# A one-core attention, expert and gated MLP kernel: exponential table and row sums of the first tiles, and the order of two accumulations

## The chip, the core and the metric

The kernel runs on one core of a Trainium2 chip. The metric is the device time of one execution in microseconds; the figure for a kernel is the median of its runs. The profile shows one such execution, instruction by instruction, on the five engines: TensorE (PE in the rows; its weight loads are PEld), VectorE (DVE), ScalarE (ACT), GpSimd (POOL) and SyncE (SP), which issues the DMAs.

## What is computed

Three stages follow each other, all in float32, on 2304 tokens of width 512 (18 tiles of 128 tokens):

```
attention, in chunks of 64 tokens, 8 heads of width 64:
    scores = q @ k.T / 8;  scores -= max(scores);  attn = exp(scores)
    attn /= sum(attn) + 1e-9;  x = attn @ v
experts, 4 of them, width 1024, p = probs normalised per token:
    out += p[:, e] * (relu(x @ w1[e]) @ w2[e])
gated MLP, width 1536:
    xn = x / sqrt(mean(x * x) + 1e-6) * rms_g
    out = (silu(xn @ w_gate) * (xn @ w_val)) @ w_out
```

## The kernel before

The 18 token tiles are worked in three sets of six. Within a set, two blocks of three tiles (384 tokens) are the columns of the first products. Every float32 matrix is split into a high and a low float32r part, and a product is the sum of three matmuls: high by high, high by low, low by high (PASSES). In the code and in the rows, hh and hl are the two parts of the hidden activations, w the two parts of a weight tile, x those of the input.

**First products.** All but the very first use a scheme with seven products per pair of chunks in place of eight (hidden, from line 738): a_ps, b_ps, d_ps and c_ps are the PSUM banks of its partial results, VectorE adds them up (line 198, a helper), ScalarE applies Relu and writes hh (line 796), VectorE writes hl (line 799). In the gated MLP VectorE multiplies by the silu (line 830), ScalarE writes hh (line 833), and hl comes from GpSimd, or, for the last chunk of the first block, from VectorE (line 197, a helper). That last chunk is the bank d_ps, the last product to end. The first set's first pair of chunks is done plainly instead (plain, bank c_ps).

**Second products.** After every two pairs of chunks (fps, k = 0 and 1, each with two chunks j) outer runs over the six token tiles t. For each tile it takes one PSUM bank, o, and adds up 12 matmuls of 128x512 (line 856): six for the pair k = 0, then six for k = 1. Then flush moves the bank out: VectorE scales it and adds it into acc (line 1049; 1047 the first time) in the expert stage, or adds it into out in the gated MLP. I call one run of outer a pass. There are 33, of 72 matmuls each: 8 for each set in the expert stage (24), 3 for each set in the gated MLP (9). They are numbered from 0.

**Lead-in.** Before the first pass the six attention tiles of the first set are computed one by one (attention_unit with first_softmax), between the plain products of the first two pairs of chunks. For a tile TensorE makes the scores (sc), VectorE takes row maxima (line 616) and the negative bias nb (line 620), ScalarE makes the exponentials, four for each half (line 625, accum_out gives the row sums as well), VectorE turns the sums into reciprocals (lines 631 and 632), GpSimd multiplies (at, line 635), TensorE transposes (trA, line 521), ScalarE copies (aT, line 526), TensorE multiplies with v (pv, line 544), and ScalarE and VectorE write the parts of x (lines 560, 197 and 571). In the same stretch ScalarE and GpSimd split the first weights, which arrive as r from in_w (ScalarE's casts are lines 315 and 356, GpSimd's subtractions line 197). TensorE fills some idle time with transposes into a bank called scratch (line 959).

**What sets the order.** The program is recorded in one go, engine by engine, in the order in which the Python code issues it; each engine then works through its own list in order. In the lead-in Chains.race decides that order: each generator says before a step which engine it needs and for how many microseconds (the dictionary in yield) and which of its own earlier steps it follows (the number), and the step that could begin first is issued first. So an estimate changed in first_softmax moves other instructions as well. Later, work.tick lets background chains (weight preparation, attention of the next sets) issue steps between the products, by a running clock. PSUM banks are handed out in the order in which they came free (Banks).

Of the kernel before, what the change touches and what calls it, by code (L numbers as in the profile page):

```python
# [8 lines left out]
F32 = mybir.dt.float32  # L9
# [3 lines left out]
AF = mybir.ActivationFunctionType  # L13
ALU = mybir.AluOpType
AX = mybir.AxisListType
# [3 lines left out]
P = 128  # L19
CH = 64  # L20

PASSES = ((0, 0), (0, 1), (1, 0))
# [128 lines left out]
def fused_kernel(ctx, tc, qkv, probs, w12, wglu, gvec, out):  # L151
# [4 lines left out]
    nc = tc.nc  # L156
# [455 lines left out]
    def first_softmax(sc, ex, att):  # L612

        mx, nb, rs = (sm.tile([P, 2, HP], F32, tag=f"f{n}", name=n) for n in ("mx", "nb", "rs"))
        for h2 in range(2):
            nc.vector.tensor_reduce(
                mx[:, h2, :].unsqueeze(2), sc[h2][:, :HP * CH].rearrange("p (g n) -> p g n", n=CH), axis=AX.X, op=ALU.max
            )
            yield {"DVE": 0.45 if h2 == 0 else 0.2}, 1
        nc.vector.tensor_scalar(nb, mx, -SCALE, None, op0=ALU.mult)  # L620
        for h2 in range(2):
            yield {"ACT": 0.9}, 1
            for g in range(HP):
                cols = slice(g * CH, (g + 1) * CH)
                nc.scalar.activation(  # L625
                    ex[h2][:, cols], sc[h2][:, cols], AF.Exp, scale=SCALE, bias=nb[:, h2, g:g + 1],
                    accum_out=rs[:, h2, g:g + 1],
                )
            banks.put(sc[h2])
        yield {"DVE": 0.5}, 1  # L630
        nc.vector.tensor_scalar_add(rs, rs, 1e-9)
        nc.vector.reciprocal(rs, rs)
        for h2, e in enumerate(ex):
            yield {"POOL": 0.65}, 1
            nc.gpsimd.tensor_tensor(
                att.rearrange("p (hp r n) -> p hp r n", hp=HP, r=2)[:, :, h2, :],
                e[:, :HP * CH].rearrange("p (g n) -> p g n", n=CH),
                rs[:, h2, :].unsqueeze(2).to_broadcast([P, HP, CH]),
                op=ALU.mult,
            )  # L640
            tp.put(e)
# [78 lines left out]
    def bank(name):  # L720
        if not banks.free():
            work.force(None, banks.free)
        return banks.get(name)
# [122 lines left out]
    def outer(fps, w2, flush, aside):  # L846

        catch_up()
        for t in range(TPS):
            b, r = divmod(t, TPB)  # L850
            ps = bank(f"o_{t}")
            last = (len(fps) - 1, 1, len(PASSES) - 1)
            for k, fp in enumerate(fps):
                for j in range(2):
                    for m, (hx, wi) in enumerate(PASSES):
                        nc.tensor.matmul(  # L856
                            ps, hs[fp, b, j][hx][:, r * P:(r + 1) * P], w2[2 * k + j][:, wi],
                            start=((k, j, m) == (0, 0, 0)), stop=((k, j, m) == last),
                        )
                if k == len(fps) - 1:  # L860
                    flush(t, ps)
                    banks.put(ps)
                work.tick(6 * 0.227)
                aside(t * UF + k)
        for fp in fps:
            for b in range(2):
                for j in range(2):
                    hi, lo = hs.pop((fp, b, j))
                    hh.put(hi)
                    hl.put(lo)  # L870
        w2p.put(*w2)
# [53 lines left out]
    with tc.manual_schedule():  # L925
        units = [[i, i + 1] for i in range(0, NTILE, 2)]
        own = lambda s: units[s * TPS // 2:(s + 1) * TPS // 2]
        make_identity(nc, ident)
        fetching = work.add(fetch())
        lead = [[i] for i in range(TPS)]  # L930
        tiles = [attention_tiles(u) for u in lead]
# [201 lines left out]
```

## Time and profile before

| | |
|---|---|
| median of 3 runs | 1246.94 us (1246.8 to 1248.53) |
| the profiled execution's own time | 1249.17 us |
| its span, first to last instruction | 1247.4 us |
| mean granted TensorE clock | 0.997 of full speed |
| PE busy, DVE busy, POOL busy, ACT busy | 1223.3, 783.0, 537.4, 449.0 us |

In timeline rows the first number is the start in microseconds from the beginning of the span, the second how long the group of instructions took, then engine, line, operation, what is written and read, shape, and how many instructions the row merges; in square brackets stands how long the engine had been idle and what ended that. A matmul's own duration is longer than the distance to the next one, since matmuls are pipelined; starts tell the pace.

### The profile page before, as it was taken

How to read it: one execution, taken by the hardware profiler on the slowest of the kernel's cores; microseconds unless marked ns; L12 is line 12 of the kernel's file. 1: busy time of each engine (PE TensorE's matmuls, PEld its weight loads, DVE VectorE, ACT ScalarE, POOL GpSimd, SP SyncE). 2: the span in 40 equal slices, each digit the busy share in tenths (PEclk: the TensorE clock that was granted, in tenths of full speed). 3: DMA queues.
4: the chain of work that ended last, by engine and by line, in shares of the span. 5: the costliest groups of instructions: out<-in, count | busy, mean ns of one | idle time of the engine just before them, and what ended most of it. 6: DMA issues, size and time to landing. Idle time of an engine off the chain costs nothing.

```text
span 1247.4 us, 20675 instructions
## 1 busy us (share of the span) xinstructions
PE 1223.3 (98%) x7253; PEld 1107.0 (89%) x7253; DVE 783.0 (63%) x1388; ACT 449.0 (36%) x1109; POOL 537.4 (43%) x575
## 2 busy tenths in 40 slices
PE   7999999999999999999999999999999999999998
PEld 6888899989997987889999999998998998998997
DVE  3765444456776787677677766786766634763644
ACT  7454333334243233333244224333435341332211
POOL 3696666654463563526355445354313101130100
PEclk9999999999999999999999999999999999999999
DMA  8377455554577697755667677657956935855843
GB/s 293 106 255 284 173 194 186 187 202 157 191 253 250 235 326 262 243 169 207 224 235 269 201 243 252 201 164 259 311 194 233 304 112 197 285 189 186 302 131 124
DMA packets 140215, 274.05 MB, mean 220 GB/s; under 512 B 16208, under 2 KB 16208, under 8 KB 140112
## 3 DMA queue, kind: packets, MB, share of 16 engines
q1 hardware_dynamic: 140112, 272.73, 64.0%
q8 instruction: 58, 0.95, 0.3%
q14 instruction: 45, 0.37, 0.1%
HBM read 210.28 MB, written 62.39 MB: 219 GB/s over the span
## 4 chain that ended last, share of the span: by engine, by line
PE 77%; DVE 8%; POOL 5%; issue 4%; ACT 3%; DMA 2%; SPq 0%; POOLq 0%; DVEq 0%
PE o L856 36%; PE d_ps L706 11%; PE a_ps L706 11%; PE c_ps L706 11%; PE b_ps L706 6%; POOL w L197 3%; DMA w1m<-w 2%; DVE silu L830 2%; POOL tw L197 1%; DVE c_ps L198 1%; PE pv L544 1%; DVE u L198 1%; ACT e L625 1%; PE xT L911 1%; PE sc L497 1%
## 5 line engine op out<-in xcount | busy, mean ns | idle before, releaser
L856 PE MATMUL o<-w,hh 128*128 128x512 f32 x1584 | 492.8, 392 | 5.3 <-ACT hh L796 3.5
L856 PEld LDWEIGHTS o<-w,hh 128*128 128x128 f32 x1584 | 295.7, 188 | 69.4 <-ACT hh L796 5.2
L856 PE MATMUL o<-w,hl 128*128 128x512 f32 x792 | 311.5, 393 | 2.2 <-DVE hl L799 1.2
L197 POOL TENSOR_TENSOR w<-r,w 128x512 fp32r<-128x512 f32 (+1 forms) x146 | 163.4, 1127 | 135.5 <-ACT w L356 76.7
L706 PE MATMUL c_ps<-x,w 128*128 128x384 f32 x1080 | 216.2, 336 | 0.3 <-ACT e L625 0.3
L706 PE MATMUL d_ps<-x,w 128*128 128x384 f32 x984 | 198.6, 336 | 2.4 <-DVE c_ps L198 2.2
L706 PE MATMUL a_ps<-x,w 128*128 128x384 f32 x984 | 198.6, 336 | 0.9 <-ACT p L759 0.9
L706 PEld LDWEIGHTS c_ps<-x,w 128*128 128x128 f32 x1080 | 188.8, 188 | 0.8 <-ACT e L625 0.5
L856 PEld LDWEIGHTS o<-w,hl 128*128 128x128 f32 x792 | 148.9, 188 | 39.2 <-DVE hl L197 4.7
L1049 DVE SCALAR_TENSOR_TENSOR acc<-o,pr,acc 128x512 f32<-128x512 f32 x126 | 94.3, 749 | 135.0 <-PE o L856 134.7
L197 POOL TENSOR_TENSOR hl<-silu,hh 128x384 fp32r<-128x384 f32 x54 | 54.4, 1030 | 288.4 <-ACT hh L833 288.3
L706 PEld LDWEIGHTS a_ps<-x,w 128*128 128x128 f32 x984 | 173.4, 188 | 3.9 <-ACT p L759 1.2
L706 PEld LDWEIGHTS d_ps<-x,w 128*128 128x128 f32 x984 | 172.1, 188 | 4.4 <-DVE c_ps L198 4.3
L198 POOL TENSOR_TENSOR w<-w,sc 128x512 f32<-128x512 f32 x36 | 47.1, 1309 | 163.0 <-DVE sc L415 139.8
L197 POOL TENSOR_TENSOR w<-tw,w 128x256 fp32r<-128x256 f32 x112 | 87.2, 787 | 39.9 <-ACT w L231 34.2
L198 DVE TENSOR_TENSOR u<-b_ps,p 128x384 f32<-128x384 f32 x82 | 45.5, 554 | 88.2 <-PE b_ps L706 46.4
L706 PE MATMUL b_ps<-x,w 128*128 128x384 f32 x492 | 99.0, 335 | 0.0
L759 ACT COPY p<-a_ps 128x384 f32<-128x384 f32 x82 | 39.5, 482 | 162.4 <-PE a_ps L706 162.3
L796 ACT ACTIVATE hh<-c_ps 128x384 fp32r<-128x384 f32 x100 | 49.1, 494 | 131.9 <-DVE c_ps L198 130.3
L198 DVE TENSOR_TENSOR u<-c_ps,u 128x384 f32<-128x384 f32 x82 | 45.6, 556 | 74.1 <-PE c_ps L706 73.5
L231 ACT CAST w<-tw 128x256 fp32r<-128x256 f32 x112 | 42.6, 406 | 136.0 <-POOL tw L197 91.4
L706 PEld LDWEIGHTS b_ps<-x,w 128*128 128x128 f32 x492 | 86.4, 188 | 0.1
(109 smaller groups left out, 1346.5 us busy)
## 6 DMA issues: line engine op xcount, KB each, us to landing
w<-wgv SPq DMA_DIRECT2D x252, 256.0 KB, 3.9
w<-w1m SPq DMA_DIRECT2D x224, 256.0 KB, 5.2
r<-in_w SPq DMA_DIRECT2D x128, 256.0 KB, 4.8
w1m<-w SPq DMA_DIRECT2D x112, 256.0 KB, 2.5
wgv<-w SPq DMA_DIRECT2D x84, 256.0 KB, 4.7
raw<-in_wglu SPq DMA_DIRECT2D x36, 512.0 KB, 3.8
w<-wou SPq DMA_DIRECT2D x36, 512.0 KB, 7.4
wou<-q SPq DMA_DIRECT2D x24, 256.0 KB, 4.4
```

The lines of the kernel that those rows point to most:

```text
L197: sub = lambda eng, o, a, b: eng.tensor_tensor(o, a, b, op=ALU.subtract)
L198: add = lambda eng, o, a, b: eng.tensor_tensor(o, a, b, op=ALU.add)
L231: nc.scalar.copy(halves(out[n])[:, 0], at[part_of[n]])
L497: nc.tensor.matmul(sc[h2][c * CH:(c + 1) * CH, n:n + CH], q, k, start=True, stop=True)
L544: nc.tensor.matmul(ps[n][lo:lo + CH, o:o + CH], vt[a][lo:lo + CH, hp, ch, :], aT[a][lo:lo + CH, q:q + CH], start=True, stop=True,)
L625: nc.scalar.activation(ex[h2][:, cols], sc[h2][:, cols], AF.Exp, scale=SCALE, bias=nb[:, h2, g:g + 1], accum_out=rs[:, h2, g:g + 1],)
L706: nc.tensor.matmul(ps[:, :NB], wv[:, wi, k, :], xs[n][:, xi, k, :], start=(first and k == 0 and m == 0), stop=(last and k == KH - 1 and m ...
L759: nc.scalar.copy(p1, v(a))
L796: nc.scalar.activation(hi, src, AF.Relu)
L830: nc.vector.tensor_tensor(v, ps[:, :NB], v, op=ALU.mult)
L856: nc.tensor.matmul(ps, hs[fp, b, j][hx][:, r * P:(r + 1) * P], w2[2 * k + j][:, wi], start=((k, j, m) == (0, 0, 0)), stop=((k, j, m) == last),
L1049: nc.vector.scalar_tensor_tensor(out=acc[i], in0=ps, scalar=pr[:, i, e:e + 1], in1=acc[i], op0=ALU.mult, op1=ALU.add,)
```

## The change

Three things are edited. In first_softmax the exponentials no longer give row sums; instead VectorE adds up each half of a tile (a new TENSOR_REDUCE for each half, 12 in all), with estimates of their own for the race. Ahead of everything, a value of one element per partition is set to zero by VectorE and passed through Exp on ScalarE. In outer, the first two token tiles take turns: tile 0 with the pair k = 0, tile 1 with k = 0, tile 0 with k = 1, tile 1 with k = 1, with two banks open; the other four tiles stand as before.

```diff
             for g in range(HP):
                 cols = slice(g * CH, (g + 1) * CH)
                 nc.scalar.activation(
-                    ex[h2][:, cols], sc[h2][:, cols], AF.Exp, scale=SCALE, bias=nb[:, h2, g:g + 1],
-                    accum_out=rs[:, h2, g:g + 1],
+                    ex[h2][:, cols], sc[h2][:, cols], AF.Exp, scale=SCALE, bias=nb[:, h2, g:g + 1]
                 )
             banks.put(sc[h2])
-        yield {"DVE": 0.5}, 1
+        for h2 in range(2):
+            yield {"DVE": 0.4 if h2 == 0 else 0.8}, 2 - h2
+            nc.vector.tensor_reduce(
+                rs[:, h2, :].unsqueeze(2), ex[h2][:, :HP * CH].rearrange("p (g n) -> p g n", n=CH), axis=AX.X, op=ALU.add
+            )
         nc.vector.tensor_scalar_add(rs, rs, 1e-9)
...
     def outer(fps, w2, flush, aside):

         catch_up()
-        for t in range(TPS):
+        last = (len(fps) - 1, 1, len(PASSES) - 1)
+        order = [(t, k) for t in range(TPS) for k in range(len(fps))]
+        order[1], order[2] = order[2], order[1]
+        open_banks = {}
+        for n, (t, k) in enumerate(order):
             b, r = divmod(t, TPB)
-            ps = bank(f"o_{t}")
-            last = (len(fps) - 1, 1, len(PASSES) - 1)
-            for k, fp in enumerate(fps):
-                for j in range(2):
-                    for m, (hx, wi) in enumerate(PASSES):
-                        nc.tensor.matmul(
-                            ps, hs[fp, b, j][hx][:, r * P:(r + 1) * P], w2[2 * k + j][:, wi],
-                            start=((k, j, m) == (0, 0, 0)), stop=((k, j, m) == last),
-                        )
-                if k == len(fps) - 1:
-                    flush(t, ps)
-                    banks.put(ps)
-                work.tick(6 * 0.227)
-                aside(t * UF + k)
+            if k == 0:
+                open_banks[t] = bank(f"o_{t}")
+            ps = open_banks[t]
+            for j in range(2):
+                for m, (hx, wi) in enumerate(PASSES):
+                    nc.tensor.matmul(
+                        ps, hs[fps[k], b, j][hx][:, r * P:(r + 1) * P], w2[2 * k + j][:, wi],
+                        start=((k, j, m) == (0, 0, 0)), stop=((k, j, m) == last), skip_group_check=True,
+                    )
+            if k == len(fps) - 1:
+                flush(t, ps)
+                banks.put(ps)
+            work.tick(6 * 0.227)
+            aside(n)
...
         make_identity(nc, ident)
+        warm = sm.tile([P, 1], F32, tag="warm", name="warm")
+        nc.vector.memset(warm, 0.0)
+        nc.scalar.activation(warm, warm, AF.Exp)
         fetching = work.add(fetch())
```

How the instructions stand is read from the built program's lists, one for each engine. They show the order, and which engines' counters an instruction waits for, and no times.

**TensorE at the beginning of a pass** (pass 26, in the gated MLP; o is the bank of a token tile, w a chunk's weight tile with its number, hh and hl the two parts of the activations). Before, all 12 matmuls of tile 0:

```order
L856 MATMUL o_10953<-w_10793,hh 128x512 [waits DMAHW7_49]
L856 MATMUL o_10953<-w_10793,hh 128x512
L856 MATMUL o_10953<-w_10793,hl 128x512 [waits Pool_49]
L856 MATMUL o_10953<-w_10795,hh 128x512 [waits DMAHW0_49]
L856 MATMUL o_10953<-w_10795,hh 128x512
L856 MATMUL o_10953<-w_10795,hl 128x512
L856 MATMUL o_10953<-w_10804,hh 128x512 [waits DMAHW1_49,Activation_49]
L856 MATMUL o_10953<-w_10804,hh 128x512
L856 MATMUL o_10953<-w_10804,hl 128x512 [waits Pool_49]
L856 MATMUL o_10953<-w_10819,hh 128x512 [waits DMAHW2_49,Activation_49]
L856 MATMUL o_10953<-w_10819,hh 128x512
L856 MATMUL o_10953<-w_10819,hl 128x512 [waits DVE_49]
```

Now, from the sixth matmul of tile 0 on (the five before it stand as they did):

```order
L863 MATMUL o_10969<-w_10811,hl 128x512
L863 MATMUL o_10979<-w_10809,hh 128x512 x2
L863 MATMUL o_10979<-w_10809,hl 128x512
L863 MATMUL o_10979<-w_10811,hh 128x512 x2
L863 MATMUL o_10979<-w_10811,hl 128x512
L863 MATMUL o_10969<-w_10820,hh 128x512 [waits DMAHW1_49,Activation_49]
L863 MATMUL o_10969<-w_10820,hh 128x512
L863 MATMUL o_10969<-w_10820,hl 128x512 [waits Pool_49]
L863 MATMUL o_10969<-w_10835,hh 128x512 [waits DMAHW2_49,Activation_49]
L863 MATMUL o_10969<-w_10835,hh 128x512
L863 MATMUL o_10969<-w_10835,hl 128x512 [waits DVE_49]
```

Six matmuls of tile 1 that wait for nothing stand ahead of the ones that wait for ScalarE, GpSimd and VectorE; the last wait is now at the 18th matmul, not the 12th.

**ScalarE at the beginning of the lead-in** (e are the exponentials, sc the scores, w and r a weight part and its source). Before:

```order
L625 ACT_TABLE_LOAD
L625 ACTIVATE e_213,rs<-sc_195,nb 128x64 x4
L625 ACTIVATE e_214,rs<-sc_196,nb 128x64 x4
L625 ACTIVATE e_249,rs<-sc_226,nb 128x64 x4
L625 ACTIVATE e_250,rs<-sc_227,nb 128x64 x4
L625 ACTIVATE e_290,rs<-sc_263,nb 128x64 x4
L526 COPY aT_323<-trA_318 128x512
L625 ACTIVATE e_291,rs<-sc_264,nb 128x64 x4
L315 CAST w_0_360<-r_0_165 128x256
```

Now:

```order
L938 ACT_TABLE_LOAD
L938 ACTIVATE warm<-warm 128x1
L625 ACTIVATE e_216<-sc_198,nb 128x64 x4
L625 ACTIVATE e_217<-sc_199,nb 128x64 x4
L315 CAST w_0_289<-r_0_168 128x256
L625 ACTIVATE e_252<-sc_229,nb 128x64 x4
L625 ACTIVATE e_253<-sc_230,nb 128x64 x4
L625 ACTIVATE e_293<-sc_266,nb 128x64 x4
L526 COPY aT_333<-trA_328 128x512
L625 ACTIVATE e_294<-sc_267,nb 128x64 x4
```

The table load stands ahead of the data, and the first weight cast has moved ahead of the second tile's exponentials; its subtraction on GpSimd, likewise, now stands ahead of the first tile's at.

**TensorE at the end of the lead-in** (pv is the last tile's product with v, c_ps the plain products). Before:

```order
L544 MATMUL pv_696<-aT_672,v_158 64x64
L706 MATMUL c_ps<-x_190,w_0_441 128x384 x6
L706 MATMUL c_ps<-x_191,w_1_637 128x384 x6
L959 MATMUL scratch<-ident 128x128
L706 MATMUL c_ps<-x_190,w_7_714 128x384 x6
L706 MATMUL c_ps<-x_191,w_2_717 128x384 x6
L706 MATMUL c_ps<-x_192,w_0_360 128x384 x6
```

Now:

```order
L544 MATMUL pv_732<-aT_714,v_161 64x64
L969 MATMUL scratch<-ident 128x128 x2
L709 MATMUL c_ps<-x_193,w_7_575 128x384 x6
L709 MATMUL c_ps<-x_194,w_2_685 128x384 x6
L709 MATMUL c_ps<-x_195,w_0_289 128x384 x6
```

Twelve plain matmuls have moved from behind the last tile's pv to places ahead of it.

## Rows read from the trace of the kernel before

**Rows 1.** The page, part 1: busy time of each engine, share of the span, instructions.
```profile
PE 1223.3 (98%) x7253; PEld 1107.0 (89%) x7253; DVE 783.0 (63%) x1388; ACT 449.0 (36%) x1109; POOL 537.4 (43%) x575
```
**Rows 2.** Waits of the weight loads, whole span: us in total, times, longest.
```profile
PEld o L856 <- ACT hh L796: 5.2, 5, 1.9
PEld o L856 <- DVE hl L197: 4.7, 9, 0.6
...
PEld o L856 <- ACT hh L833: 2.8, 9, 0.8
PEld o L856 <- POOL w L197: 1.9, 2, 1.2
```
**Rows 3.** Timeline of PE, beginning of pass 3: tile 0's first, tile 1's first matmuls.
```profile
159.22 0.63 PE L856 MATMUL o<-w,hh 128*128 128x512 f32 x2
...
161.98 0.62 PE L856 MATMUL o<-w,hh 128*128 128x512 f32 x2
```
**Rows 4.** Timeline of PE, beginning of pass 26: first, 12th and 13th matmul.
```profile
947.75 0.63 PE L856 MATMUL o<-w,hh 128*128 128x512 f32 x2
...
950.64 0.50 PE L856 MATMUL o<-w,hl 128*128 128x512 f32 x1
950.98 0.63 PE L856 MATMUL o<-w,hh 128*128 128x512 f32 x2
```
**Rows 5.** Timeline, pass 10: first, 13th and 22nd matmul.
```profile
377.38 0.63 PE L856 MATMUL o<-w,hh 128*128 128x512 f32 x2
...
382.86 1.05 PE L856 MATMUL o<-w,hh 128*128 128x512 f32 x2
...
386.35 0.63 PE L856 MATMUL o<-w,hh 128*128 128x512 f32 x2
```
**Rows 6.** Two stretches: length, busy us (instructions) of each engine, PEclk, DMA, GB/s.
```profile
382.53:385.94 3.41, 3.41 (x9) 2.64 (x10) 2.58 (x6) 2.45 (x4) 0.00 (x0) 0.50 1.06 401
385.94:1246.00 860.06, 851.92 (x4722) 775.38 (x4720) 563.91 (x975) 284.15 (x641) 303.72 (x290) 1.00 0.66 224
```
**Rows 7.** Timeline, pass 13: first matmul, attention's transposes, first matmul of tile 1.
```profile
481.22 0.63 PE L856 MATMUL o<-w,hh 128*128 128x512 f32 x2
...
486.22 0.60 PE L521 MATMUL trA<-ident,at 128*128 128x128 f32 x4
...
486.57 0.71 PE L856 MATMUL o<-w,hh 128*128 128x512 f32 x2
```
**Rows 8.** Timeline of PE, pass 0: first matmul, first of tile 1.
```profile
47.14 0.63 PE L856 MATMUL o<-w,hh 128*128 128x512 f32 x2
...
52.01 0.63 PE L856 MATMUL o<-w,hh 128*128 128x512 f32 x2
```
**Rows 9.** Timeline of ScalarE, behind pass 0: a weight cast that waits for GpSimd.
```profile
68.44 0.41 ACT L231 CAST w<-tw 128x256 fp32r<-128x256 f32 x1 [2.84 <-POOL tw L197]
```
**Rows 10.** Timeline, pass 1: transposes of the attention, behind tile 1's first six matmuls.
```profile
87.64 0.42 PEld L521 LDWEIGHTS trA<-ident,at 128*128 128x128 f32 x4 [0.34 <-POOL at L604]
```
**Rows 11.** Timeline, the first tile: table load, an exponential, its sum's reading, the next.
```profile
5.94 1.28 ACT L625 ACT_TABLE_LOAD   x1 [5.94 <-DVE nb L620]
...
7.23 0.31 ACT L625 ACTIVATE e<-sc,nb 128x64 f32<-128x64 f32 x1
...
7.45 0.19 ACT L625 ACTIVATION_READ_ACCUMULATOR e<-sc,nb 128x1 f32 x1
7.54 0.31 ACT L625 ACTIVATE e<-sc,nb 128x64 f32<-128x64 f32 x1
...
10.30 1.18 POOL L635 TENSOR_TENSOR at<-e,rs 128x256 f32<-128x256 f32 x2 [9.00 <-DVE rs L632]
```
**Rows 12.** Groups by line and form: count, busy us, mean ns of one, idle before.
```profile
L616 DVE TENSOR_REDUCE mx<-sc 128x4 f32<-128x256 f32 x12 | 4.4, 410 | 8.6 <-PE sc L497 8.6
```
**Rows 13.** The same view, whole span: row sums of later tiles, read from SBUF.
```profile
L599 DVE TENSOR_REDUCE rs<-e 128x8 f32<-128x512 f32 x12 | 8.1, 672 | 0.0
```
**Rows 14.** Timeline of PE, end of the lead-in: plain products behind the last pv.
```profile
36.63 10.67 PE L706 MATMUL c_ps<-x,w 128*128 128x384 f32 x60
```

## The prediction, made before the changed kernel ran

> **What bounds the kernel now.** I read the page first. TensorE is busy for 98% of the span [rows 1], so the kernel is as long as TensorE's list plus what TensorE waits for, and faster work on another engine counts only where TensorE stands for it. Next I read the view of waits, for the weight loads, which show when TensorE would have gone on [rows 2]. The largest entries are passes that wait for the activations of the chunk that ended last: hh from ScalarE, hl from VectorE. In 9 cases the one that is late is VectorE's hl of the gated MLP, once for each of its passes. Then I read the timeline of single passes. In pass 3, which waits for nothing, tile 1's first matmul starts 2.76 us after tile 0's [rows 3]: 12 matmuls, 0.23 us each, six in 1.38 us. A pass that waits shows the excess over 2.76 us between the same two rows.
>
> **Part 1: two tiles take turns.** It adds no instruction. It puts six matmuls of tile 1 that have all they need ahead of tile 0's second half, so what that half needs may come 1.38 us later. The operands' own times hang on the first products, VectorE and ScalarE, none of which waits for the second products here. So each pass gains the smaller of its excess and 1.38 us.
>
> Pass 26: the 12th matmul starts at 950.64 and the 13th at 950.98, 3.23 us after 947.75 [rows 4]. Excess 0.47 us, all of it covered. The nine passes of the gated MLP together wait 4.7 us for hl and 2.8 us for hh by their weight loads [rows 2], 0.83 us a pass against about 0.8 in pass 26, so the pass shown is typical, slightly on the low side. I take 9 x 0.5 = **4.5 us** (4.2 to 4.8).
>
> Pass 10: 5.48 us from 377.38 to 382.86 [rows 5], excess 2.72, so 1.38 us are gained. What follows depends on the clock. From 382.53 to 385.94 the granted clock is 0.50, the 1.2 GHz level [rows 6], right behind the waits; the nine matmuls from 382.86 to 386.35 [rows 5] take 3.49 us where 9 x 0.23 = 2.07 would do, so it costs 1.42 us. In the new order half of the idle time ahead of it is filled with matmuls. Pass 13, later on, has 2.2 us of excess and no such stretch (the clock is 1.00 from 385.94 on [rows 6]), and about 1.3 us of excess are left here. I take the stretch as gone: 1.38 + 1.42 = **2.8 us**, 1.4 if it stays.
>
> Pass 13: 5.35 us from 481.22 to 486.57, with four transposes from 486.22 on between [rows 7]; without their 0.35 us the excess is 2.2, so **1.4 us**. The transposes keep their place behind the 12th matmul and then fall into the wait that is left, so it could be 1.7.
>
> Pass 0: 4.87 us from 47.14 to 52.01 [rows 8], excess 2.1. Here the late operand is a weight part from GpSimd, the only two such waits [rows 2]. It starts behind ScalarE's cast, and that behind the plain products, so it keeps its distance to the pass: 1.38 us. But behind this pass ScalarE stands 2.84 us for GpSimd's next weights [rows 9], with a copy out of a first product's bank queued behind that cast, on which VectorE and then TensorE depend. GpSimd's weights do not come earlier with this gain, so part of it is given back there. I take **1.0 us** (0 to 1.4).
>
> Pass 1 also has a long wait for hh, but behind tile 1's first half come transposes of the attention, which waited for GpSimd's at already before [rows 10]. Its multiplications hang on VectorE's reciprocals, not on TensorE, so TensorE would come earlier and stand there: **0.1 us** (0 to 1.4).
>
> Flushes stay as many. Tile 0's comes 1.38 us later, and VectorE is free for 37% of the span [rows 1], which hides that; if it were not so, one VectorE accumulation would delay a chain behind it in each pass, and I leave that to the range.
>
> **Part 2: the table.** The table load takes 1.28 us, and the first exponential starts 0.01 us after its end [rows 11]. Ahead of the data it costs nothing, because ScalarE had been idle for 5.94 us [rows 11]. The first exponentials start about 1.3 us earlier. The Trainium skill (ScalarE: Activation LUTs, What ACT_TABLE_LOAD costs) counts about 1.28 us for the load and 1.38 us more for a drain, 2.66 us for each switch. By that the first tile would gain 2.7 us. The trace has the 1.28 and no drain between the load and the exponential [rows 11], and I go by it.
>
> **Part 3: the sums.** From an exponential's start to its sum's reading it is 0.22 us, from there to the next exponential 0.09 us [rows 11]. Without the reading the pace is between 0.22 and 0.31, and I take the former, since the reading has a slot of its own: 48 x 0.09 = 4.3 us less on ScalarE. For them VectorE gets 12 reductions. A reduction of this shape from PSUM takes 0.41 us [rows 12], one of twice the length from SBUF 0.67 [rows 13], so 0.34 to 0.41, some 4.9 us. Per tile ScalarE saves 0.7 us and the last half's sum adds 0.4 us behind it, so a tile's reciprocals come about 0.3 us earlier, and TensorE gains less than the 4.3 us.
>
> The order takes some of it back. The first weight cast now stands ahead of the second tile's exponentials and its subtraction ahead of the first at; that at stands at 10.30 us [rows 11] and can hardly come earlier, so the first tile keeps little of the table's gain. Later, the fourth tile's aT copy stands ahead of the last tile's exponentials. The other way, twelve plain matmuls move from behind the last pv to ahead of it. Sixty take 10.67 us [rows 14], so twelve are 2.1 us less between the last pv and pass 0. The last pv itself can come up to 1 us earlier or up to 2 us later, by those two moves. I take **1.2 us** for the lead-in; the bounds are 0 and 3.1.
>
> **Sum.** 4.5 + 2.8 + 1.4 + 1.0 + 0.1 + 1.2 = 11.0 us. The profiled execution took 1249.17 us, so 1238.2 by its account. The median of the runs is 2.2 us below that execution, 1246.94, and gives **1235.9 us**, which I forecast.
>
> **Rivals.**
> 1. The low clock stays in pass 10, or comes back elsewhere: 9.6 us are gained, 1237.3. For it: what the clock answers to can't be read from one stretch. Against it: pass 13 waited nearly as long without it [rows 6, 7]. Chance 0.13.
> 2. In the expert stage and the lead-in the waits only move. GpSimd and VectorE work in a chain there [rows 9, 10], and TensorE meets the next wait earlier. Then the gated MLP's 4.5 us alone are left, 1242.4. For it: pass 1. Against it: no other pass shows attention waiting right behind its excess. Chance 0.08.
> 3. Nothing stays, within 2.5 us: the lead-in loses what the passes gain. It would have to lose over 7 us, more than all added sums. Chance 0.04.
> 4. Slower: the second open bank. If the bank for tile 1 is one that the last chunk has just left, TensorE waits for VectorE's hl at the seventh matmul instead of the 12th. In pass 26 that hl lets the 12th matmul start 2.89 us behind the first [rows 4]; the seventh would be due at 1.38, so it would stand 1.5 us where 0.5 stood, 1.0 us more, 33 us over all passes: 1280. It decides from the point at which fewer banks than two have been free for longer than a chunk's time. Against it: banks go round in the order in which they came free, and the list of pass 26 shows no wait at tile 1's first matmul. Chance 0.02.
> 5. The alternation itself brings the clock down. A low stretch costs 1.4 us [rows 5]; one in each pass would be 47 us, 1294. Each token tile has a bank of its own already, and only pass 10 shows a low stretch at its beginning, behind waits that get shorter. The Trainium skill (TensorE: Matmul & The Clock Gate, A second HAM failure mode: psum-queue depth-cycling) speaks against this change: a kernel that cycled through PSUM banks idled briefly between groups, and its clock went up and down. By that rule the banks should cost here already; the clock is full from 385.94 on [rows 6], over 22 passes. Chance 0.01.
>
> **How the numbers follow.** The forecast has the remaining 0.72. The range takes in it and rival 1: at its low end all upper bounds (4.8 + 2.8 + 1.7 + 1.4 + 1.4 + 3.1 = 15.2, 1231.7), at its high end the low clock and a lead-in and pass 0 that give nothing (4.2 + 1.4 + 1.4 = 7.0, 1239.9) with 1 us for a flush in the way: 1231.5 to 1241.0. Left out are rivals 2 to 5, 0.15. Of no change this kernel's measurement can tell about 0.2%, 2.5 us. Faster than that are the forecast and rivals 1 and 2, 0.93; the same is rival 3, 0.04; slower are rivals 4 and 5, 0.03.
>
> **What would show it.** In the profile after: the table load near 1 us and the first exponential near 6; pass 0 starting 0 to 3 us before 47.14; in the gated MLP's passes no wait of line 863's loads for hl, and 18 matmuls in 4.1 us; between the last pv and pass 0 sixty plain matmuls, in 10.7 us; clock 1.00 through pass 10. A wait for VectorE at the seventh matmul of a pass would make it wrong, as would transposes of the attention that take over the excess in pass 13 or behind pass 0.

## The result, and the profile after

| | time |
|---|---|
| changed kernel, median of 4 runs | 1233.28 us (1233.2 to 1234.68) |
| kernel before, the same series | 1246.87 us (1246.09 to 1248.53) |
| ratio | 0.9887, 95% interval 0.9873 to 0.9902 |
| profiled execution of the changed kernel | 1233.29 us, span 1231.5 us |

The changed kernel is 13.6 us faster in medians; 11.0 were forecast, and 1233.28 lies in the range. A second series of the same kernel (e8 below) gave 1233.97. The two profiled executions differ by 15.9 us of span (1247.4 and 1231.5), more than the medians, and that difference turned out to be worth looking at.

The page, part 1, answers to [rows 1]: VectorE has 13 instructions more, ScalarE 47 fewer, and TensorE is busy 99% of a shorter span.

```profile
PE 1214.6 (99%) x7254; PEld 1105.5 (90%) x7254; DVE 787.2 (64%) x1401; ACT 444.9 (36%) x1062; POOL 538.5 (44%) x575
```

The view of waits of the weight loads answers to [rows 2] (us in total, times, longest):

```profile
PEld trA L521 <- POOL at L604: 2.9, 3, 1.6
...
PEld a_ps L709 <- ACT p L762: 2.0, 2, 1.2
PEld o L863 <- ACT hh L799: 1.7, 3, 0.8
...
PEld o L863 <- POOL w L197: 1.4, 2, 1.0
```

The two rows of the gated MLP, nine waits for VectorE's hl and nine for ScalarE's hh, are gone altogether. The first two rows shown have taken over something: transposes of the attention waited 1.6 us for GpSimd's at before, now 2.9, and the loads of a_ps waited 1.2 us for the copy p, now 2.0.

The timeline of PE, pass 26, answers to [rows 4]: first, 13th and 19th matmul.

```profile
935.86 0.62 PE L863 MATMUL o<-w,hh 128*128 128x512 f32 x2
...
938.59 0.62 PE L863 MATMUL o<-w,hh 128*128 128x512 f32 x2
...
939.95 0.39 PE L863 MATMUL o<-w,hh 128*128 128x512 f32 x1
```

2.73 us to the 13th, 4.09 to the 19th: no wait. All nine passes of the gated MLP look like this.

The timeline of PE, pass 10, answers to [rows 5]:

```profile
373.20 0.63 PE L863 MATMUL o<-w,hh 128*128 128x512 f32 x2
...
376.66 0.50 PE L863 MATMUL o<-w,hl 128*128 128x512 f32 x1
377.66 0.73 PE L863 MATMUL o<-w,hh 128*128 128x512 f32 x2 [0.49 <-ACT hh L799]
```

Two stretches of the view by windows, pass 10's beginning and what follows (columns as in [rows 6]):

```profile
373.20:378.50 5.30, 4.70 (x19) 3.18 (x19) 3.70 (x8) 2.37 (x5) 1.73 (x2) 1.00 1.06 386
378.50:405.00 26.50, 26.50 (x137) 24.35 (x137) 19.38 (x37) 10.08 (x19) 9.16 (x7) 1.00 0.81 274
```

The wait now stands behind the 15th matmul, 1.3 us of excess are left, and the granted clock is 1.00 throughout, the 2.4 GHz level.

The timeline behind pass 0, ScalarE first and then PE: the place of [rows 9].

```profile
65.67 0.41 ACT L231 CAST w<-tw 128x256 fp32r<-128x256 f32 x1 [2.85 <-POOL tw L197]
65.98 0.47 ACT L762 COPY p<-a_ps 128x384 f32<-128x384 f32 x1
...
66.51 1.31 PE L709 MATMUL a_ps<-x,w 128*128 128x384 f32 x6 [0.48 <-ACT p L762]
```

The copy stands behind the cast, and a first product behind the copy: 0.64 us over its usual pace, where the kernel before had no wait.

The lead-in: timelines of ScalarE, GpSimd and PE, to be read beside [rows 11], [rows 14] and [rows 8].

```profile
0.73 1.28 ACT L938 ACT_TABLE_LOAD   x1 [0.73 <-PEq L1132]
...
5.96 1.75 ACT L625 ACTIVATE e<-sc,nb 128x64 f32<-128x64 f32 x8 [3.73 <-DVE nb L620]
...
9.97 1.18 POOL L638 TENSOR_TENSOR at<-e,rs 128x256 f32<-128x256 f32 x2
...
33.72 10.64 PE L709 MATMUL c_ps<-x,w 128*128 128x384 f32 x60
44.20 0.62 PE L863 MATMUL o<-w,hh 128*128 128x512 f32 x2
```

The first exponential starts at 5.96 instead of 7.23, eight take 1.75 us (0.22 each, the value taken), the first at comes only 0.33 us earlier, and pass 0 starts 2.94 us earlier than 47.14.

By stretches from one pass's first matmul to the next, the two profiled executions differ so:

| stretch | before | after | gain | forecast |
|---|---|---|---|---|
| start to pass 0 | 47.14 | 44.20 | 2.94 | 1.2 |
| pass 0 to 1 | 34.39 | 34.11 | 0.28 | 1.0 |
| pass 1 to 2 | 42.16 | 41.87 | 0.29 | 0.1 |
| pass 10 to 11 | 35.14 | 32.18 | 2.96 | 2.8 |
| pass 13 to 14 | 41.33 | 39.41 | 1.92 | 1.4 |
| gated MLP (pass 24 to the end) | 395.2 | 389.5 | 5.7 | 4.5 |
| the remaining 20 passes | | | 1.75 | 0 |

Nearly each of the 20 gains 0.05 us even where it waits for nothing on either side; that is about 1.1 of the 1.75. Most of the rest lies in passes 8, 12 and 19, which waited 0.1 to 0.2 us for a late operand before and wait no more. No term of the prediction stands for either.

### The profile page after: what moved, and what is told of

The parts are those of the page before. It is cut to its first block, busy times and chain, and to the rows that moved or that the text cites. A ratio compares the mean times of both kernels' runs of the same rounds, so it can differ in the third digit from the quotient of the medians.

```text
span 1231.5 us, 20640 instructions
## 1 busy us (share of the span) xinstructions
PE 1214.6 (99%) x7254; PEld 1105.5 (90%) x7254; DVE 787.2 (64%) x1401; ACT 444.9 (36%) x1062; POOL 538.5 (44%) x575
## 4 chain that ended last, share of the span: by engine, by line
PE 87%; DVE 4%; POOL 3%; issue 2%; ACT 2%; DMA 2%; SPq 0%; POOLq 0%; DVEq 0%; ACTq 0%
PE o L863 41%; PE d_ps L709 13%; PE a_ps L709 12%; PE c_ps L709 12%; PE b_ps L709 6%; POOL w L197 1%; DMA w1m<-w 1%; PE pv L544 1%; POOL tw L197 1%; PE xT L918 1%; DVE c_ps L198 1%; DVE hl L802 0%; DVE s L197 0%; DVE u L198 0%; PE trA L521 0%
```

## The experiments

The theory: late operands keep their own times, so a pass gains the smaller of its excess and 1.38 us; the lead-in gains by table and sums together. The rivals: waits only move; the table is all of the lead-in's gain. Then come the 0.05 us, and what is left to gain. Each was timed against the kernel before on the same chip; "below" is the difference of medians.

### The four parts alone

e1 is the kernel before with the new `outer` alone:

```diff
-        for t in range(TPS):
...
+        order = [(t, k) for t in range(TPS) for k in range(len(fps))]
+        order[1], order[2] = order[2], order[1]
+        open_banks = {}
+        for n, (t, k) in enumerate(order):
```

> The kernel before with the alternating order of the second products alone; lead-in as before. Theory (late operands keep their own times, so each pass gains the smaller of its excess and 1.38 us): gated MLP -5.8 us as in the profile after (9 x 0.6), pass 10 -1.4 (-3.0 if the kernel before has its low clock there in its ordinary runs too), pass 13 -1.4 to -1.9, passes 0 and 1 together -0.6, small waits of other passes up to -1.7: between -9.2 and -11.5 us against the kernel before. Pass 0 starts at 47.1 us in its profile, not at 44.2. Rival A (in the expert stage the waits only move, and the profile after shows it otherwise only because the lead-in shifted the whole schedule): -5 to -6 us, the gated MLP alone. Rival B (two open banks cost something in each pass): less than the sum of the passes' excess, matmuls of the first two tiles longer than before.

Measured: 1237.35 us, 9.96 below (ratio 0.9927, 0.9914 to 0.9939). The five terms on the passes had 9.8 together. The gated MLP takes 390.1 us (5.0 less), pass 10 to 11 32.25, pass 13 to 14 39.45: the passes gain by themselves, and rival A falls. So does rival B: the undisturbed period is 30.95 us as before. What the profile adds, first the timeline of PE at the beginning of pass 0:

```profile
45.80 0.39 PE L860 MATMUL o<-w,hh 128*128 128x512 f32 x1
```

and a window in pass 1 of the same execution:

```profile
86.30:89.71 3.41, 3.25 (x10) 2.77 (x11) 0.00 (x0) 1.21 (x4) 3.33 (x6) 0.50 0.00 0
```

With the old lead-in pass 0 starts at 45.80 here, not at 47.14, and a stretch at half clock stands in pass 1, behind TensorE's wait for GpSimd's at, where the kernel before had none.

e2 has the lead-in of the change (`first_softmax` and the early exponential) and the old passes:

```diff
-                    accum_out=rs[:, h2, g:g + 1],
...
+            nc.vector.tensor_reduce(
+                rs[:, h2, :].unsqueeze(2), ex[h2][:, :HP * CH].rearrange("p (g n) -> p g n", n=CH), axis=AX.X, op=ALU.add
+            )
...
+        warm = sm.tile([P, 1], F32, tag="warm", name="warm")
+        nc.vector.memset(warm, 0.0)
+        nc.scalar.activation(warm, warm, AF.Exp)
```

> The kernel before with the early table and the row sums on VectorE alone; second products in the old order. Theory (the two parts add up): pass 0 starts near 44.2 us in its profile, 2.9 us earlier than 47.14, and the whole is -2 to -3 us; passes 10 and 13 and the gated MLP keep their excess. Rival A (without the alternation pass 0 waits longer for GpSimd's weight part, since it starts earlier and GpSimd is not earlier): 0 to -1.5 us, with the excess of pass 0 above 2.1 us. Rival B (the gain of the lead-in needs the clock to be full from 9 us on, which is chance): -1 to -3 us, and a stretch of granted clock 0.50 in the lead-in.

Measured: 1244.56 us, 2.75 below (0.9981, 0.9972 to 0.999), as the theory had it, but pass 0 starts at 46.21, not near 44.2. The same 15 transposes ahead of the first at tell why; the timeline of PE of e2:

```profile
9.57 3.46 PE L965 MATMUL scratch<-ident 128*128 128x128 f32 x15
```

The same of the changed kernel:

```profile
9.19 1.86 PE L969 MATMUL scratch<-ident 128*128 128x128 f32 x15
```

The same matmuls take 1.9 times as long, about the ratio of the two levels, so in e2's profiled execution TensorE seems to have been at its lower level still. (The trace's record of the granted clock begins at 13.69 us in e2 and at 8.99 in the changed kernel, both at 1.00; nothing is recorded before that, so the lower level is inferred from the durations.) When the clock comes up in the lead-in then differs from execution to execution, and a single profile's start of pass 0 is uncertain by more than the lead-in term.

e3 is the early exponential alone (the last three lines of the diff above).

> The kernel before with one exponential of one column ahead of the data, so that the table load lies in ScalarE's idle time; row sums on ScalarE as before. Theory: the first exponential starts about 1.3 us earlier (near 6.0 us in its profile), the first tile's aT up to 1.3 us earlier, later tiles less, since each waits for its own scores and for VectorE: 0 to -1.3 us in all. Rival (a drain of 1.38 us goes with the load, as the Trainium skill has it): the first exponential 2.7 us earlier. Second rival (the whole gain of the lead-in, 2.9 us, is the table): -2.5 to -3 us.

Measured: 1245.03 us, 2.28 below (0.9982, 0.9973 to 0.9991): too much for the theory, by time near the second rival. The timelines of ScalarE and PE say otherwise:

```profile
0.73 1.28 ACT L931 ACT_TABLE_LOAD   x1 [0.73 <-PEq L1125]
...
6.00 0.31 ACT L625 ACTIVATE e<-sc,nb 128x64 f32<-128x64 f32 x1 [3.77 <-DVE nb L620]
...
19.09 1.09 PE L544 MATMUL pv<-aT,v 64*64 64x64 f32 x30 [1.48 <-ACT aT L526]
```

The first exponential is 1.23 us earlier, the load's own 1.28 and no more, so the first rival falls; for the drain that the Trainium skill (ScalarE: Activation LUTs, What ACT_TABLE_LOAD costs) adds to a load there is no room here. But by the third tile TensorE waits 1.48 us for ScalarE (0.78 in the changed kernel and e1), and pass 0 starts at 45.52. So little of the 2.28 lies in the lead-in; most of it lies in the 0.05 us of each pass, which e3 has and e1 has not.

e4 has the row sums on VectorE alone (the first part of e2's diff).

> The kernel before with the row sums of the first tiles on VectorE alone; the table load stays ahead of the first exponential, near 6 us. Theory (what the table does not bring, the sums and the order that they lead to bring: twelve plain matmuls move from behind the last pv to ahead of it): -1.3 to -2.9 us, pass 0 starting between 44.2 and 45.8 us. Rival (VectorE's 12 reductions lengthen its chain, and without the early table nothing is left): 0 to +1 us, the first at later than 10.30 us by a reduction, 0.4 us.

Measured: 1246.64 us, 0.67 below, ratio 1.0 (0.9991 to 1.0009): no difference that can be told. The theory fell by time. Pass 0 starts at 45.00, which is 0.5 to 0.8 us earlier than in e6 (45.51) and e1 (45.80); but the record of the clock also begins earlier here, at 8.67 us against 9.88 and 11.20, so not all of that need be the sums. The profiled execution has two stretches at half clock (windows):

```profile
49.63:53.05 3.42, 3.42 (x10) 2.67 (x9) 2.49 (x3) 0.57 (x2) 3.34 (x5) 0.50 0.00 0
380.73:384.14 3.41, 3.27 (x8) 2.59 (x9) 3.23 (x8) 1.65 (x4) 0.00 (x0) 0.50 1.01 374
```

Without the share of the moved buffers, some 1.65 us (next section), the medians give about 0.6 us for the table, 0.67 for the sums and 1.1 for both, each uncertain by about 1 us: they add up as far as can be told. That the table alone makes ScalarE the bound at the third tile is seen in e3; that each part needs the other is not shown. With both, pass 0 starts at 44.00 to 44.95 in eight profiles, 44.2 in their middle (46.21 in e2), against 45.51 and 45.80 with the old lead-in and no low stretch in it. Those are 1.3 to 1.6 us, but in both of the latter the clock's record begins late. e1 and e7 (the change with the buffers unmoved), whose records begin alike at 11.20 and 11.17 us, start pass 0 at 45.80 and 44.95, 0.85 apart. The medians on this chip differ by 0.8 us (e1 and e7) and 1.3 (e6 and e2). So the lead-in is worth some 0.8 to 1.3 us, where 1.2 were forecast.

### The 0.05 us of every pass

The changed kernel, e2 and e3 have it; the kernel before, e1 and e4 do not. What the first three share is the new tile. `sm` has six buffers for each tag and lies ahead of all pools of the weights and of hh and hl, so a tag of 4 bytes moves all these by 6 x 32 = 192 bytes. e6 allocates the tile and leaves the exponential away; e7 is the changed kernel with the exponential on a column that exists already:

```diff
 e6, against the kernel before
+        warm = sm.tile([P, 1], F32, tag="warm", name="warm")
+        nc.vector.memset(warm, 0.0)
 e7, against the changed kernel
-        warm = sm.tile([P, 1], F32, tag="warm", name="warm")
+        warm = psm[:, 0]
```

> The kernel before with the one-column tile allocated and set to zero, and no exponential on it: no table moves. It is for the small gain in all undisturbed passes (30.94 to 30.89 us a pass with its products) that the three kernels with the early table show in their profiles and the three without it do not: in the latter the nine matmuls behind each change from first to second products start 229, 233, 236, 224, 231, 236, 228, 232, 231 ns apart, in the former 229, 233, 231 and then 227. Theory (it comes from the tile's allocation, which moves every later buffer in SBUF): the pass period is 30.89 us and the time 1.0 to 1.7 us below the kernel before. Rival A (it comes from the early table): period 30.94 and no difference. Rival B (it is a property of an execution or of the day): either, without regard to the kernel.

> The changed kernel with the early exponential on a column of a constant tile that is overwritten later, so that the new tile is not allocated and buffers lie where they lay before; the table is as early as in the changed kernel. Theory (the small gain in all passes comes from the allocation): the pass period is 30.94 us as before, and the time 1.7 us above the changed kernel's, 1234.5 to 1235.5. Rival A (it comes from the early table): period 30.89, same time as the changed kernel. Rival B (a property of an execution): either.

e8 is the changed kernel once more.

> The changed kernel itself on the same chip, to compare the three others with, and to see how often its executions show a stretch at half the granted clock. Theory (such a stretch follows where TensorE stood waiting, and the change takes the longest waits away): 1233.2 to 1234.7 us, most executions without one, against none to two in those of the kernel before. Rival (they come as often as before, and the changed kernel's profile happened to show none): a spread of 1233 to 1237 us, like the 1245.3 to 1249.1 of the kernel before.

Measured: e6 1245.87, 0.97 below (0.9986, 0.9977 to 0.9995); e7 1236.55 (0.9915, 0.9901 to 0.9928); e8 1233.97 (0.9895, 0.9881 to 0.9908). The starts of passes 16 and 17 in the timeline of PE, e6:

```profile
583.13 0.39 PE L856 MATMUL o<-w,hh 128*128 128x512 f32 x1
...
614.03 0.39 PE L856 MATMUL o<-w,hh 128*128 128x512 f32 x1
```

and e7:

```profile
578.80 0.39 PE L863 MATMUL o<-w,hh 128*128 128x512 f32 x1
...
609.75 0.39 PE L863 MATMUL o<-w,hh 128*128 128x512 f32 x1
```

30.90 and 30.95 us (starts are rounded to 0.01): the short period comes with the allocation, without any table, and goes with it, with the table. Both rivals fall. 33 passes times 0.05 are 1.65 us. From pass 2 to the end the profile of e7 takes 1113.3 us and that of e8 1111.4, 1.9 apart; those of the kernel before and e6, pass 10 left out, 1088.5 and 1086.9, 1.6 apart. Of the gains of e2 and e3, 2.75 and 2.28, that is more than half. In medians e6 shows less (0.97) and e7 more (2.6, and 1.0 above its theory); the spread of their runs, 1.6 to 3.5 us, may account for that, and no run settles it.

e8 also answers the question of the clock. Its runs go from 1233.26 to 1234.79, three of four with a mean clock of 1.000. Of the 27 runs of the kernel before beside e1 to e4, six had 1.000 (1245.26 to 1246.06 us), three 0.997 (1248.91 to 1249.09). In the profiles with the old passes, three of five have the low stretch in pass 10; of the nine with the new order none, and three of those have one in pass 1. Over all kernels, the mean clock was 0.998 or less in 3 of 38 runs with the new order (two of them of e10, below) and in 29 of 71 with the old one (these 27 and the runs of e2, e3, e4 and e6). The theory holds: with the new order such stretches are rarer in these runs, and not gone.

### What is left to gain

e5: three tiles take turns.

```diff
-        order[1], order[2] = order[2], order[1]
+        order[:6] = [(t, k) for k in range(2) for t in range(3)]
```

> The changed kernel with three token tiles taking turns: 18 matmuls of the first chunk pair ahead of the first that needs the second pair. Theory (what is left of a pass's excess is the late operand's lateness beyond 1.38 us, and another 1.38 us of matmuls ahead of it hides it): excess left in the changed kernel's profile is 1.15 us in pass 0, 1.30 in pass 10, 1.28 in pass 13; pass 10 and 13 lose all of theirs, 2.6 us; of pass 0's most is given back behind it: 2.5 to 3.5 us below the changed kernel, 1230 to 1231 us. Rival (the passes 0, 1 and 13 are bound by VectorE's and GpSimd's chains, so the wait comes again at the attention's transposes or the next first product): pass 10's 1.3 us alone, 1232. Second rival (a third open bank is one that is not free in time): slower than the changed kernel, with a wait at the 13th matmul of every pass.

Measured: 1232.54 us (0.9884, 0.9868 to 0.9899), 1.4 below e8 on the same chip, its four runs all below e8's four. Pass 10 to 11 takes 30.91 us, no wait left; pass 13 to 14 38.97, 0.4 less. Pass 0 loses its excess, and then (timeline of PE):

```profile
66.18 1.31 PE L709 MATMUL a_ps<-x,w 128*128 128x384 f32 x6 [1.41 <-ACT p L762]
...
83.86 0.66 PE L521 MATMUL trA<-ident,at 128*128 128x128 f32 x4 [1.62 <-POOL at L604]
```

The product's lag grew from 0.64 to 1.57: 0.93 of the 1.13 us are given back at the next wait. So the rival was right for pass 0, and the theory for pass 10; the gain lies between the two. The second rival falls: no wait at a 13th matmul.

e9 takes the place of the copy away: the first copy p<-a_ps goes to VectorE, in the changed kernel. e10 does the same in e5.

```diff
-        nc.scalar.copy(p1, v(a))
+        (nc.scalar.copy if firsts else nc.vector.tensor_copy)(p1, v(a))
+        firsts.append(key)
```

> The changed kernel with the very first copy p<-a_ps, behind pass 0, on VectorE instead of ScalarE, so that it does not stand behind the cast that waits for GpSimd's weights. Two token tiles take turns as in the changed kernel. Theory (behind pass 0 GpSimd's chain sets the pace, so the wait only moves on): the wait of the a_ps product, 0.64 us in the changed kernel's profile, is gone, and the wait of pass 1's transposes for GpSimd's at grows from 1.3 to 1.6 by as much, to 1.9 to 2.2: 0 to 0.2 us gained, median 1233.5 to 1234. Rival (the copy's place behind the cast is itself what gives the gain back): 0.5 to 0.7 us gained, 1233.3, with the transposes' wait as it was.

> Three token tiles take turns and the first copy p<-a_ps is on VectorE. With three tiles alone, pass 0's excess fell from 1.15 to 0.01 us, and the wait of the a_ps product behind it rose from 0.64 to 1.57. Theory (GpSimd's chain sets the pace behind pass 0): the 1.57 us go on to the wait of pass 1's transposes, 1.78 with three tiles alone, which comes to about 3.3; pass 2 starts where it did, 75.7 us behind pass 0, and the time is that of three tiles alone, 1232.0 to 1232.6. Rival (the copy's place): pass 2 starts 1.5 us earlier, 1231.

Measured: e9 1234.07 us (0.9893, 0.988 to 0.9907), e8's time; e10 1232.24 (0.9883, 0.9867 to 0.99), e5's. In e9 the product's wait is gone, and the theory's sum holds, but its place was wrong: the transposes wait 1.3 as before, and pass 1's 16th matmul waits 1.44 for hh where it waited 0.63 in e8. In e10 it is the transposes, 3.35 us. The timelines of VectorE and GpSimd in pass 1, changed kernel:

```profile
79.97 0.60 DVE L600 TENSOR_SCALAR rs<-rs 128x8 f32<-128x8 f32 x1
...
79.22 1.32 POOL L197 TENSOR_TENSOR w<-r,w 128x512 fp32r<-128x512 f32 x1
```

and e9:

```profile
79.57 1.76 DVE L600 TENSOR_SCALAR rs<-rs 128x8 f32<-128x8 f32 x1
...
79.33 1.28 POOL L197 TENSOR_TENSOR w<-r,w 128x512 fp32r<-128x512 f32 x1
80.58 0.72 POOL L197 TENSOR_TENSOR w<-tw,w 128x256 fp32r<-128x256 f32 x1
```

In e8, the changed kernel once more, the same operation took 1.28 us, so a part of what differs between e9's profile and the changed kernel's is no work of the edit; and e10's pass 1 has a stretch at half clock, from 83.79 us on, so that pass 2 starts 76.4 us behind pass 0 there, not 75.7.

VectorE's operation on eight columns ends at 80.57 and 81.33, each 0.03 us behind the end of one of GpSimd's (80.54, 81.30), in e9 the second that ends after its start; the next of its kind, where GpSimd does nothing, takes 0.17. The reciprocal, the last addition and the last two hl stand behind it on VectorE, and hh of the last product behind that addition. By these rows GpSimd's weights set the pace of pass 1, whatever is done ahead. The Trainium skill (SBUF — State Buffer, Who interferes with whom) states that VectorE and GpSimd share a pair of ports, that a tensor_scalar can claim it where its operands allow, and that the one who comes second is blocked for the other's whole instruction. The rows agree, and the operation stood longer than that in e9 and e8, through the rest of one of GpSimd's and the whole of the next. Moving that operation was not tried, so the cause is argued from the rows and not shown by a run.

### Where the buffers lie

e11 (on e5) pads the new tile so that all buffers behind x begin at multiples of 512 bytes; e12 pads ahead of x, so that x does too.

```diff
 e11
+    gap = ctx.enter_context(tc.tile_pool(name="gap", bufs=1))
...
+        warm = gap.tile([P, 120], F32, name="warm")[:, :1]
 e12
+    gap = const.tile([P, 120], F32, name="gap")
...
+        warm = gap[:, :1]
```

> Three tiles take turns, and the new tile is a padded one of 480 bytes in a pool of its own instead of six buffers of 32 bytes, so that all later buffers lie at multiples of 512 bytes in SBUF, where the kernel before has them 32 bytes behind one and the changed kernel 224. Theory (any place other than the old one gives the shorter succession 229, 233, 231, 227): the pass period stays 30.89, time as with three tiles alone, 1232 to 1232.6. Rival A (a boundary of 512 bytes is best): all matmuls behind the change of product at 227, period 30.87 or less, 0.5 to 1 us less. Rival B (what matters is something else that moved with the buffers): period 30.94, 1.7 us more.

> Three tiles take turns; the 480 bytes of padding now lie ahead of the activations x too, so that x and all later buffers begin at multiples of 512 bytes. In the kernel before all of them lay 32 bytes behind such a boundary; in the changed kernel x at 32 and the later ones at 224; in the run with 480 bytes behind x, x at 32 and the later ones at 0, and there a first product's matmuls started 174 to 180 ns apart instead of 173 to 174 (pass period 31.16 us instead of 30.89) while the second products lost the slow beginning. Theory A (what slows the first products is where x and the weights lie towards each other): period 30.94 at most, since x and weights lie towards each other as in the kernel before: 1232 to 1234.3 us. Theory B (the boundary itself, at which the weights begin, slows them): period 31.16, 1239 to 1240 us. The third possibility (a boundary is best if all buffers begin on one): period below 30.89, 1231 to 1232.

Measured: e11 1239.47 us (0.9936, 0.9924 to 0.9948), 7 us above e5 and above e10, which ran on the same chip; e12 1234.34 (0.9894, 0.9877 to 0.9911). No theory of e11 had that. Two first products between passes 16 and 17 in the timeline of PE, e11:

```profile
595.07 1.22 PE L710 MATMUL a_ps<-x,w 128*128 128x384 f32 x6
596.13 1.22 PE L710 MATMUL b_ps<-x,w 128*128 128x384 f32 x6
```

and the changed kernel:

```profile
593.88 1.20 PE L709 MATMUL a_ps<-x,w 128*128 128x384 f32 x6
594.92 1.20 PE L709 MATMUL b_ps<-x,w 128*128 128x384 f32 x6
```

1.06 us for each product of six matmuls against 1.04, so 14.84 us for the 14 products of a pass against 14.56, and 31.16 for its period. In e12, with the same boundary for the weights, it is 30.94 again: what counts is where x and the later buffers lie towards each other, as theory A had it. The distances, modulo 512 bytes: 0 in the kernel before and e12 (30.94), 192 in the changed kernel (30.89), 480 in e11 (31.16). Only these three were run. In e12 x and the later buffers lie exactly as far apart as in the kernel before, so whether 512 bytes are the measure is not shown. Nor are a matmul's own two operands the whole of it: in pass 16 half of the 0.05 us lies in the 72 second products (16.13 us from the first start to the last in the kernel before, 16.11 in the changed kernel), half in the 84 matmuls of the first ones (14.41 and 14.39), and the operands of the second products, w and the parts of the hidden activations, moved together.

## Why the prediction was right

**The passes.** Right in mechanism: with the new order alone (e1) the waits are gone or shorter where they were priced. In sum 9.8 were forecast and 9.96 measured (7.6 to 10.7 by the interval of the ratio). That the two agree so well is in part luck: pass 0 was 0.7 too high, the gated MLP and pass 13 0.5 too low each, passes 8, 12 and 19 not in the sum with 0.5, and pass 10's low stretch was counted in full though only some executions have it.

- Gated MLP, 4.5: without the buffers' share 5.0. The failed step is "the pass shown is typical": passes 24 and 25 had an excess of 0.66 and 0.80 us, the other seven 0.47. The waits by weight loads [rows 2], 0.83 a pass against 0.8, pointed that way.
- Pass 10, 2.8: 2.96, of which 1.3 are turns and 1.6 the low stretch (35.14 against 33.55 and 33.56 in e2 and e6, which have the old order and no low stretch there). But that stretch is in some executions only, so in a median the term is worth less than 1.4. And it was counted on top of "The median of the runs is 2.2 us below that execution": those 2.2 us are in part the same low stretches, of which the profiled execution of before had two, in the lead-in and here.
- Pass 13, 1.4 to 1.7: 1.92, and 1.88 in e1. From its first matmul to the 19th it took 7.19 us before and takes 5.37 now: 1.38 and the 0.35 of the transposes, which fell into the wait, as said, make up nearly all of that.
- Pass 0, 1.0: 0.28. At the pass itself 1.0 was gained (excess 2.1 before, 1.1 after), and 0.64 went again at the next first product. The give-back was named with its place and came there; it was under-sized. e5 shows the rate: 0.93 of 1.13.
- Pass 1, 0.1: 0.29, within its bounds by luck: in e8, the same kernel, the pass takes 42.56 us, 0.40 more than before. The wait for hh (1.47 before) went over to the transposes (1.29, for at), as said.

**The lead-in.** 1.2 forecast, 0.8 to 1.3 by e1 with e7 and e6 with e2, each uncertain by about 1 us. The 2.94 of the two profiled executions holds the one that the kernel before had in its lead-in in that execution. Twelve plain matmuls did move ahead of the last pv, which came 0.88 us earlier. No drain came with the table.

**What no term held.** 1.6 to 1.9 us by moved buffers; the forecast of 11.0 fell short of the measured 13.6 mostly by that. "It costs nothing" was said of the table, and the tile for it was looked at as an instruction, not as an allocation.

**The rivals.** 2 and 3 fall with e1. Rival 1 is right in part: the low clock left pass 10, but in three of nine profiles came back in pass 1, behind waits that did not get shorter there. Rival 4: no pass of any profile waits at its seventh matmul. Rival 5: in e1 the undisturbed passes keep their period and a clock of 1.00; what low stretches are left stand behind waits.

## What to carry to other kernels

A pass that waits for its last operand gains the smaller of its excess and of the work that can be put ahead; then look at who stands next in the queue of the engine that was late, since there the gain is given back. Before a profile's low-clock stretch or its lead-in is priced, compare a second execution of the same kernel. And a new tile moves every buffer behind it: a control that allocates it and does nothing else tells that share.

## What was not expected of the hardware

TensorE's pace changed with the distance in SBUF between the input x and the buffers behind it: 1.04 or 1.06 us for six matmuls of a first product, and 0.05 us more or less a pass, half in the first and half in the second products; up to 7 us over this kernel (1232.54 and 1239.47). Why, no run here tells. One operation of VectorE on eight columns took 0.17 to 1.76 us, by what GpSimd did at that time. And stretches of 3.41 us at the 1.2 GHz level come in some executions and not in others of the same kernel, behind waits of TensorE, for some 1.4 to 1.6 us each.

The fastest of these kernels is the change with three tiles in turn, with or without the copy on VectorE: 1232.54 and 1232.24 us, not to be told apart.
